# A decode attention block with a gated MLP: TensorE's program made shorter, the first key transpose of unit 1 moved ahead of unit 0's softmax, and the gate moved on VectorE

## The chip, the cores and the metric

One core of one Trainium2 chip runs the kernel. The metric is the device time of one execution in microseconds (us). The kernel before has a median of 111.82 us over 14 runs (111.16 to 113.61).

## The reference

```
x = A_x                                   # [2, 1, 448], bfloat16
xn = layernorm(x)
q = xn @ wq                               # 16 heads of 256
k, v = the last 2048 positions of k_cache, v_cache   # 8 kv heads, each serves 2 q heads
o = softmax(q k^T / 16) v
s = o @ wo                                # [2, 1, 448]
g = silu(relu(xn @ w1) @ w2)              # 448 -> 1792 -> 448
out = x + s * g
```

Two tokens are computed (batch 2), so each weight and each cached key or value is used once or twice: 44 MB are read and hardly any arithmetic is done with them.

## The kernel before

**Units.** The attention is cut into four units, u = 0 to 3: unit u is batch u // 2 and the four kv heads of half u % 2. A unit has 4 MiB of keys and 4 MiB of values. Partition 32h + r holds head h and, for r, 64 neighbouring positions of 256 numbers each (`kv_src`, line 274).

**A unit's work.** VectorE (DVE) transposes the keys in four blocks, `do_T` (376), 32 x 32 at a time, into `kt`. TensorE multiplies each block with the query `qz` in `do_S` (383), eight matmuls in four column tiles, into the bank `sbk`. `softmax` (400) takes the maximum on DVE, the exponential on ScalarE (ACT, 407), a second DVE transpose (409), 16 matmuls that spread the result (413) and a product with a mask (417), which leaves the weights in `pt`; the sum for the denominator is a matmul with `gsum` (420). `do_PV` (426) is 32 matmuls of `pt` with the values. `attend_scale` (443) divides by the sum into `o_sb`; `attend_turn` (448) and `attend_spread` (461) are five small matmuls and two DVE steps that lay the result out in `at_z`, as the stationary operand for wo. `turn_q` (393) writes the next unit's query.

**Loop on TensorE.** `turn(u)` (528) is written four times for the other engines, but TensorE's instructions are put in a loop of four turns by `_Prog.run` (46), with parts in branches (`turn`, `spread`, `pv`, `ffn`), each emitted once. Within the loop a wait is a token: the giver adds to a semaphore and TensorE takes away (102). Turn u does the transposes and scores of unit u, then PV of unit u - 1, then softmax u. PV of unit 3 and the end stand after the loop. A block `pe_visit` (153) is jumped to first and jumps back. All DVE instructions are a single list in the order in which they are written.

**Queries and MLP.** `do_q` (469) needs all of wq and the normalised x (`xr`, 366). `do_H` (483) has x as the stationary operand and w1 as the moving one, in turn 1; its result is clipped, transposed and copied on DVE (491 to 495) and is the stationary operand of `do_F` (509), 14 matmuls on w2 in four column tiles. Their four partial sums are folded at the end (582), and the gate (583, 605 to 608) is computed in a layout of 8 rows by 112 columns.

**The wo product.** `do_wo` (587): nine of the 32 row blocks run as four column tiles into `obk`, are copied (603) and folded into `hbk`; the other 23 add four matmuls of 112 columns each (596). The last two DVE steps (611, 613) make `out_sb`, and ACT's queue writes it.

**Loads.** All large loads are issued by the SP queue, in this order, each behind its wait: wq's first part, K0, wq's rest, K1, V0, w1, w2; K2 (after the scores of unit 0, since K0 and K2 share a buffer); V1 (after PV of unit 0) and K3 (scores of unit 1); V2 (PV of unit 1) and V3 in two parts into the buffer that wq had; then wo in seven parts of 9, 7, 5, 4, 3, 2 and 2 row blocks, after the scores of unit 2, into K0's and K2's buffer.

Of the kernel before, what the change touches and what calls it, by code (L numbers as in the profile page):

```python
# [14 lines left out]
class _Op:  # L15
    __slots__ = ("eng", "fn", "deps", "dma", "needed", "value", "sem", "turn", "group", "token", "gives")

    def __init__(self, eng, fn, deps, dma):
        self.eng, self.fn, self.deps, self.dma = eng, fn, deps, dma
        self.needed, self.value, self.sem = dma, 0, None  # L20
        self.turn, self.group, self.token, self.gives = None, None, None, False


class _Prog:
# [4 lines left out]
    def __init__(self, nc, es):  # L29
        self.nc, self.es = nc, es  # L30
        self.lists = {PE: [], DVE: [], ACTE: [], SP: [], POOL: []}
        self.turn, self.group, self.runs = None, None, {}

    def op(self, eng, fn, deps=(), token=None):
        o = _Op(eng, fn, [d for d in deps if d is not None], False)
        if eng == PE:
            o.turn, o.group, o.token = self.turn, self.group, token
        self.lists[eng].append(o)
        return o
# [6 lines left out]
    def run(self, turns):  # L46
# [6 lines left out]
        taken = {DVE: [], SP: []}  # L53
        for o in pe:
            if o.token is not None:
                assert not o.token.gives
                o.token.gives = True
                taken[o.token.eng].append(o.token)
        for e in taken:
            assert taken[e] == [o for o in self.lists[e] if o.gives]  # L60
# [16 lines left out]
        for e, ops in self.lists.items():  # L77
            sem, count = self.es.enter_context(nc.semaphore(f"s_{e}")), 0
            for o in ops:
                if o.gives:  # L80
                    assert o.dma or not o.needed
                    o.sem = give[e]
# [3 lines left out]
                elif o.needed:  # L86
                    count += 1
                    o.sem, o.value = sem, count
# [22 lines left out]
        for eng, name in ((nc.vector, "dve"), (nc.tensor, "pe")):  # L111
            again[name] = eng.alloc_register(f"{name}_again")
            nc.br("dve_all" if name == "dve" else "pe_visit", engines=[eng.engine])
# [15 lines left out]
        body = [o for o in loop if o.turn == turns - 1]  # L129
        body += [o for o in loop if o.group == "ffn"]  # L130
        with nc.body("pe_all", parent=main, valid_engines=[t.engine]):
            top = nc.cur_bb
# [3 lines left out]
            with t.Fori(0, turns) as i:  # L136
                k = 0
                while k < len(body):
                    g = body[k].group
                    end = next((m for m in range(k, len(body)) if body[m].group != g), len(body))  # L140
                    part, runs = body[k:end], self.runs[g]
                    k = end
                    if runs == list(range(turns)):
                        emit(t, part, seen)
                    elif len(runs) == 1:
                        with t.If(i == runs[0]):
                            emit(t, part, seen)
                    else:
                        assert runs == list(range(runs[0], turns))
                        with t.If(i > runs[0] - 1):  # L150
                            emit(t, part, seen)
            nc.br("pe_past", engines=[t.engine])
            nc.switch_bb("pe_visit", parent=main)
            t.nop()
            nc.br("pe_all", engines=[t.engine])
            nc.switch_bb("pe_past", parent=top)
# [5 lines left out]
def bass_recurrent_scan__sliding_block_cached__dense_activation_relu__decode_kernel(  # L162
# [21 lines left out]
    NU = 4  # L184
# [9 lines left out]
    FIRST = 2  # L194
    NCOL = D // 4
    NROW = 4 * B
    GAP = NROW + 3
    es = contextlib.ExitStack()
    with es:
# [31 lines left out]
        q_n = named("q_n", [128, 512], BF)  # L231
        qz = named("qz", [128, 4 * 64], BF)
        h_n = named("h_n", [128, FC // 4], BF)
        h_t = named("h_t", [128, FC // 4], BF)
        h_z = named("h_z", [128, 14 * GAP], BF)
        x_c = named("x_c", [NROW, NCOL], BF)
        ea = named("ea", [NROW, NCOL], F32)
        g_sb = named("g_sb", [NROW, NCOL], F32)
        tmp = named("tmp", [NROW, NCOL], F32)
# [8 lines left out]
        q_t = named("q_t", [128, 512], F32)  # L248
        ssum = named("ssum", [128, 1], F32)
# [15 lines left out]
        obk_last = psum("obk_last", [128, 512], F32)  # L265
# [13 lines left out]
        d_xc = pr.dma(ACTE, x_c[:, :], A_x[:, 0, :].rearrange("b (i n) -> (b i) n", i=4))  # L279

# [13 lines left out]
        def load_v(u, cuts=(0, NT)):  # L294
            deps = [None if u == 0 else st["q_mm"] if u == NU - 1 else st["PV", u - 1]]
            d_v[u] = []
            for lo, hi in zip(cuts, cuts[1:]):
                d_v[u].append((hi, pr.dma(SP, vbuf[u // (NU - 1)][:, lo * DH:hi * DH],
                                          kv_src(u, A_v_cache)[:, :, lo * DH:hi * DH], deps)))

        d_wq = [pr.dma(SP, wq_sb[:, 0:FIRST * HC], wq_src[:, 0:FIRST * HC])]
        load_k(0)
        d_wq.append(pr.dma(SP, wq_sb[:, FIRST * HC:SLOTS * HC], wq_src[:, FIRST * HC:SLOTS * HC]))
        load_k(1)
        load_v(0)
        st["w1"] = pr.dma(SP, w1_sb[:, 0:W2_AT], w1_src)
        st["w2"] = pr.dma(SP, w2_sb[:, W2_AT:W2_AT + 14 * D].rearrange("p (hf f) -> p hf f", hf=2), w2_src)
# [5 lines left out]
        p_z = [pr.op(POOL, lambda e, t=t: e.memset(t[:, :], 0.0)) for t in (qrep, spread, sel, h_z, at_z)][-1]  # L313

        a_z = [pr.op(ACTE, lambda e, t=t: e.memzero(t[:, :])) for t in (obk, sbk, hbk, fbk, obk_last)][-1]
# [7 lines left out]
        pr.op(ACTE, lambda e: e.activation(tmp[0:B, 0:1], st2[0:B, 0:1], ACT.Exp), [a_sd])  # L323
        for e2 in range(2):
# [39 lines left out]
        for s in range(SLOTS):  # L364
            m_xr = pr.op(PE, mm(mbk_ap(2 * s, 2), xg[0:B, 128 * s + 128:128 * s + 256], ident[0:B, 0:B], s == 0),
                         [v_xn, p_id])
# [56 lines left out]
        def out_bank(u):  # L423
            return obk if u < NU - 1 else obk_last

        def do_PV(u, gs=range(4)):
            bank, src = out_bank(u), vbuf[u // (NU - 1)]
            for g in gs:
                deps, token = [], None
                if u == NU - 1:  # L430
                    deps = [next(d for hi, d in d_v[u] if hi >= 16 * g + 16), st["pt", u]]
                elif g == 0:
                    token = d_v[u][0][1]
                for a in range(2):
                    for i in range(4):
                        t = 16 * g + 4 * i + 2 * a
                        o = pr.op(PE, mm(bank[32 * i:32 * i + 16, :],
                                         pt[:, 8 * t:8 * t + 16], src[:, t * DH:(t + 2) * DH],
                                         g == 0 and a == 0, g == 3 and a == 1, tile_position=(0, 32 * i)), deps, token=token)
                        deps, token = [], None  # L440
            st["PV", u] = o

        def attend_scale(u):
            st["osb", u] = pr.op(DVE, lambda e: e.tensor_scalar(  # L444
                out=o_sb[:, :], in0=view(out_bank(u), 0, [[1, 512]]), scalar1=rs[:, u:u + 1], scalar2=None, op0=ALU.mult),
                [st["PV", u], st["rs", u], st.get(("oT", u - 1))])

        def attend_turn(u):
            deps = [st["osb", u]] if u > 1 else []
            for dhi in range(2):  # L450
                for tp in range(2):
                    o = pr.op(PE, mm(mbk_ap(136 + 8 * dhi, 8), o_sb[:, 256 * tp + 128 * dhi:256 * tp + 128 * dhi + 128],
                                     fold[:, 8 * tp:8 * tp + 8], tp == 0, tp == 1), deps)
                    deps = []
# [6 lines left out]
        def attend_spread(u):  # L461
# [3 lines left out]
                                      [at] if u > 1 else [], token=None if u > 1 else at)  # L465
# [3 lines left out]
        def do_q():  # L469
            deps = d_wq + [v_xr, a_z]  # L470
# [6 lines left out]
            st["q_mm"] = o  # L477
# [5 lines left out]
        def do_H():  # L483
            deps = [st["w1"]]
            for s in range(SLOTS):
                for i in range(4):
                    lo = s * FC + i * (FC // 4)
                    o = pr.op(PE, mm(hbk[32 * i:32 * i + 4, 0:FC // 4], xr[:, 4 * s:4 * s + 4], w1_sb[:, lo:lo + FC // 4],
                                     s == 0, s == SLOTS - 1, tile_position=(0, 32 * i)), deps)
                    deps = []  # L490
            v = pr.op(DVE, lambda e: e.tensor_scalar(
                out=h_n[:, :], in0=hbk[:, 0:FC // 4], scalar1=0.0, scalar2=None, op0=ALU.max), [o])
            v = pr.op(DVE, lambda e: e.transpose(h_t[:, :], view(h_n, 0, [[1, 7], [7, 32]])), [v])
            st["h"] = pr.op(DVE, lambda e: e.tensor_copy(
                view(h_z, 3, [[GAP, 7], [7 * GAP, 2], [4, 2]]), view(h_t, 0, [[32, 7], [2, 2], [1, 2]])), [v, p_z])
# [13 lines left out]
        def do_F():  # L509
            deps = [st["w2"], st["h"]]  # L510
            for f in range(14):
                st["F"] = tiled(fbk, h_z, f, w2_sb, W2_AT + f * D, 4, 10, deps)
                deps = []

        def idle_work(n, deps=()):
            for _ in range(n):
                pr.op(PE, mm(wbk[:, :], ident[:, :], q_n[:, :], True, True), deps)
                deps = ()

        def idle_loop(n, m):  # L520
            def fn(e):
                with e.Fori(0, n):
                    for _ in range(m):
                        o = mm(wbk[:, :], ident[:, :], q_n[:, :], True, True)(e)
                return o
            pr.op(PE, fn)

        def turn(u):
            pr.turn, pr.group = u, "all"
            for blk in range(NBLK):  # L530
                if u:
                    do_T(u, blk)
                if u > 1 and blk in (1, 2):
                    pr.group = "turn" if blk == 1 else "spread"
                    (attend_turn if blk == 1 else attend_spread)(u - 2)
                    pr.group = "all"
# [109 lines left out]
```

## Time and profile before

| | |
|---|---|
| median of 14 runs | 111.82 us |
| the profiled execution | 111.83 us, its span 110.4 us |
| DMA | 44.11 MB, 94.8% of the 16 engines' span, 400 GB/s over it |
| VectorE busy | 63.0 us (57%), 96 instructions |
| TensorE busy | 59.8 us (54%), 552 matmuls |
| ScalarE, GpSimd busy | 10.2 us, 3.1 us |
| TensorE clock granted, mean | 0.86 of full speed |
| a key transpose, 128x2048 | 2.28 us, 16 of them |

The span is the stretch that the profile covers; the rest of an execution's time lies around it. A row of the profile names an instruction's line, engine and tiles, how often it ran, and how long its engine had been idle before it and for what. A line that a helper shares, such as 361 for every matmul, is told apart by its tiles. The chain of waits is followed back from the last instruction: at each step to what released it.

### The profile page before, as it was taken

To read this page: it belongs to the slowest core of one execution; us is meant where nothing else is said; L and a number is where in the kernel's file an instruction comes from. 1 tells how busy PE (TensorE), PEld (TensorE's weight loads), DVE (VectorE), ACT (ScalarE), POOL (GpSimd) and SP (SyncE) were. 2 spreads that over 40 slices of the span, in tenths; PEclk is the share of its full clock that TensorE was granted. 3 is DMA by queue.
4 is the path that set the end of the run, shared out by engine and by line. 5 is a ranking of instruction groups with operands and counts; after the bars stand their busy time and mean duration, and the time that the engine had idled before them with its cause. 6 is when DMAs were issued, how large, how long until landed. Compare 5 with 4: busy or idle time off the path is not lost. (4 is left out here: it accounts for less than half of the span.)

```text
span 110.4 us, 1362 instructions
## 1 busy us (share of the span) xinstructions
PE 59.8 (54%) x552; PEld 19.6 (18%) x558; DVE 63.0 (57%) x96; ACT 10.2 (9%) x19; POOL 3.1 (3%) x11
## 2 busy tenths in 40 slices
PE   0001000075799032999553597992049785888993
PEld 0000000020110030002241010131001022534792
DVE  2049109997200569992586999256399925714601
ACT  4990000000000200000200000020000002000000
POOL 7400000000000000000000000000000000000000
PEclk9999999999769955559998559678558999999999
DMA  3999989998999899998999999899899999899940
GB/s 72 485 389 463 475 358 453 484 428 380 439 487 404 380 397 409 407 520 380 487 451 392 392 523 416 380 428 487 309 439 392 442 428 428 377 423 414 399 178 1
DMA packets 3045, 44.13 MB, mean 400 GB/s; under 512 B 354, under 2 KB 612, under 8 KB 1508
## 3 DMA queue, kind: packets, MB, share of 16 engines
q1 hardware_dynamic: 3008, 44.11, 94.8%
q8 instruction: 1, 0.02, 0.1%
q10 hardware_dynamic: 36, 0.01, 0.0%
HBM read 44.11 MB, written 0.00 MB: 400 GB/s over the span
## 5 line engine op out<-in xcount | busy, mean ns | idle before, releaser
L379 DVE STREAM_TRANSPOSE kt<-kbuf 128x2048 f32<-128x2048 f32 x16 | 35.9, 2286 | 8.6 <-DMA kbuf<-in_A_k_cache_dram 8.6
L361 PE MATMUL sbk<-kt,qz 128*8 128x512 bf16 x128 | 31.1, 1072 | 14.8 <-PEq L102 14.7
L401 DVE TENSOR_REDUCE rm<-sbk 128x1 f32<-128x512 f32 x4 | 2.8, 692 | 14.3 <-PE sbk L361 14.3
L361 PE MATMUL obk<-vbuf,xr 128*4 128x512 bf16 x28 | 3.0, 598 | 14.0 <-DMA vbuf<-in_A_wq_dram 14.0
L407 ACT ACTIVATE et<-sbk,bias 128x512 bf16<-128x512 f32 x4 | 2.7, 687 | 81.2 <-DVE bias L405 81.2
L361 PEld LDWEIGHTS sbk<-kt,qz 128*8 128x8 bf16 x128 | 2.4, 87 | 29.6 <-issue 29.5
L361 PE MATMUL obk<-vbuf,pt 128*16 128x512 bf16 x96 | 6.9, 437 | 0.0
L361 PE MATMUL pbk<-et,spread 128*128 128x32 bf16 x64 | 2.6, 193 | 6.1 <-PEq L102 6.1
L361 PE MATMUL mbk<-ident,xg 2*128 2x2 bf16 x7 | 0.3, 163 | 8.5 <-DVE xg L325 8.5
L361 PE MATMUL hbk<-kbuf,at_z 128*8 128x112 bf16 x92 | 4.8, 213 | 0.0
L409 DVE STREAM_TRANSPOSE et<-et 128x512 bf16<-128x512 bf16 x4 | 2.8, 712 | 3.4 <-ACT et L407 3.4
L417 DVE TENSOR_TENSOR pt<-pbk,hmask 128x512 bf16<-128x512 f32 x4 | 2.8, 692 | 3.3 <-PE pbk L361 3.3
L361 PEld LDWEIGHTS hbk<-kbuf,at_z 128*8 128x8 bf16 x92 | 4.6, 87 | 0.1
L361 PE MATMUL wbk<-q_n,ident 128*128 128x512 bf16 x9 | 3.3, 381 | 2.0 <-DVE qz L396 1.4
L361 PEld LDWEIGHTS obk<-vbuf,pt 128*16 128x16 bf16 x96 | 2.7, 104 | 7.7 <-issue 6.3
L361 PEld LDWEIGHTS pbk<-et,spread 128*128 128x128 bf16 x64 | 2.2, 102 | 9.3 <-issue 9.3
L361 PEld LDWEIGHTS obk<-vbuf,xr 128*4 128x4 bf16 x28 | 0.8, 114 | 15.5 <-issue 15.5
L611 DVE TENSOR_TENSOR tmp<-hbk,g_sb 8x112 f32<-8x112 f32 x1 | 0.3, 262 | 4.4 <-PE hbk L361 4.4
L456 DVE TENSOR_TENSOR at_exp<-mbk,qmask 128x128 bf16<-128x128 f32 x4 | 1.2, 292 | 2.5 <-PE mbk L361 2.5
L361 PE MATMUL obk_last<-vbuf,pt 128*16 128x512 bf16 x32 | 2.3, 380 | 0.3 <-DMA vbuf<-in_A_v_cache_dram 0.3
L322 DVE RECIPROCAL rstd<-sd 2x1 f32<-2x1 f32 x1 | 0.2, 151 | 4.0 <-ACT sd L321 4.0
L444 DVE TENSOR_SCALAR o_sb<-obk,rs 128x512 bf16<-128x512 f32 x3 | 2.2, 731 | 0.0
(80 smaller groups left out, 44.7 us busy)
## 6 DMA issues: line engine op xcount, KB each, us to landing
kbuf<-in_A_k_cache_dram SPq DMA_DIRECT2D x4, 4096.0 KB, 24.1
vbuf<-in_A_v_cache_dram SPq DMA_DIRECT2D x3, 4096.0 KB, 15.6
wf<-in_B_w_dram SPq DMA_DIRECT2D x2, 1568.0 KB, 43.0
vbuf<-in_A_v_cache_dram SPq DMA_DIRECT2D x1, 3072.0 KB, 21.9
vbuf<-in_A_wq_dram SPq DMA_DIRECT2D x1, 2560.0 KB, 20.9
vbuf<-in_A_wq_dram SPq DMA_DIRECT2D x1, 1024.0 KB, 6.2
vbuf<-in_A_v_cache_dram SPq DMA_DIRECT2D x1, 1024.0 KB, 23.7
kbuf<-in_A_wo_dram SPq DMA_DIRECT2D x1, 1008.0 KB, 25.5
```

The source lines that it names most:

```text
L322: v_rs = pr.op(DVE, lambda e: e.reciprocal(rstd[0:B, :], sd[0:B, 1:2]), [a_sd])
L361: return lambda e: e.matmul(out_ap, lhsT=lhsT, rhs=rhs, start=start, stop=stop, skip_group_check=True, **kw)
L379: st["kt", u, blk] = pr.op(DVE, lambda e: e.transpose(view(dst, 0, [[1, 32 * NT]]), view(src, 32 * blk, [[DH // 2, NT], [1, 32]])), [d_k[u ...
L401: v = pr.op(DVE, lambda e: e.tensor_reduce(out=rm[:, :], in_=sbk[:, :], axis=AX.X, op=ALU.max), [st["S", u, NBLK - 1]])
L407: a = st["exp", u] = pr.op(ACTE, lambda e: e.activation(e_sb, sbk[:, :], ACT.Exp, bias=bias[:, 0:1], accum_out=ssum[:, 0:1]), [v, st.get(( ...
L409: token = pr.op(DVE, lambda e: e.transpose(e_t, e_sb), [a, st.get(("Pt", u - 1))])
L417: st["pt", u] = pr.op(DVE, lambda e: e.tensor_tensor(out=view(pt, 0, [[8, NT], [2, 4], [1, 2]]), in0=view(pbk, 0, [[2, NT], [0, 4], [1, 2] ...
L444: st["osb", u] = pr.op(DVE, lambda e: e.tensor_scalar(out=o_sb[:, :], in0=view(out_bank(u), 0, [[1, 512]]), scalar1=rs[:, u:u + 1], scalar ...
L456: st["at", u] = pr.op(DVE, lambda e: e.tensor_tensor(out=view(at_exp, 0, [[16, 8], [8, 2], [1, 8]]), in0=view(mbk, 136, [[1, 8], [8, 2], [ ...
L611: v_t = pr.op(DVE, lambda e: e.tensor_tensor(out=tmp[:, :], in0=hbk[0:NROW, 0:NCOL], in1=g_sb[:, :], op=ALU.mult), [m_o, v_g])
```

## The change

- **Program of TensorE.** The block that was visited first is gone. The loop runs six turns instead of four, with its parts in the order `turn`, `ffn`, `s`, `pv`, `softmax`, each in a branch: PV of unit 3 and the last two attend steps are turns 4 and 5 of the loop. The matmuls for `xr` and H become loops over the seven slots with computed addresses. More waits of TensorE become tokens.
- **First transpose of unit 1.** In turn 0 `do_T(1, 0)` is issued after the scores of unit 0 and ahead of softmax 0; turn 1 transposes blocks 1 to 3 only. `attend_turn` and `attend_spread` of unit u - 2 now stand ahead of turn u's transposes and scores instead of between them.
- **MLP.** H has w1 as the stationary operand (128 columns, seven elements apart) and runs right after q; one DVE step clips its result into `h_z` behind the second transpose of unit 0. F is 14 matmuls of 448 columns in one tile and moves to turn 4. The gate works on 2 rows by 448 columns, and on DVE it stands behind the copy of wo's first sums and ahead of `o_sb` of unit 3.
- **wo.** The first nine blocks and their fold are in turn 4 (`early_wo`), in a bank of their own. The others are two matmuls of 224 columns in two column tiles. Output and x are two rows at partition 0 and two at 32, and the output is written by two DMAs, from ACT and SP.
- **Loads.** wq in one piece, w1, K0, K1, V0, K2, V1, K3, V2, w2, wo's first part, V3 (in the buffer of the other V, after PV of unit 2), wo's other parts. V0 to V2 get a second, 64-byte load for the second token.
- **Fillers.** Two matmuls on a spare bank ahead of each softmax's matmuls and two behind them; a filler loop of two rounds ahead of PV 3 (five before).

```
-        d_wq = [pr.dma(SP, wq_sb[:, 0:FIRST * HC], wq_src[:, 0:FIRST * HC])]
+        d_wq = pr.dma(SP, wq_sb[:, 0:SLOTS * HC], wq_src)
+        st["w1"] = pr.dma(SP, w1_sb[:, 0:W2_AT], w1_src)
         load_k(0)
-        d_wq.append(pr.dma(SP, wq_sb[:, FIRST * HC:SLOTS * HC], wq_src[:, FIRST * HC:SLOTS * HC]))
         load_k(1)
         load_v(0)
...
         def do_H():
+            def body(e, s):
+                for j in range(7):
+                    o = mm(view(hbk, 64 + 4 * j, [[1, 4]]), view(w1_sb, FC * s + j, [[7, 128]]), view(xr, 4 * s, [[1, 4]]), False)(e)
+                return o
+            return looped(SLOTS, body, [st["w1"]])
...
         def do_F():
             deps = [st["w2"], st["h"]]
             for f in range(14):
-                st["F"] = tiled(fbk, h_z, f, w2_sb, W2_AT + f * D, 4, 10, deps)
+                st["F"] = pr.op(PE, mm(view(fbk, 0, [[1, D]], n=B), view(h_z, f * GAP + 3, [[4, 2]]),
+                                       w2_sb[:, W2_AT + f * D:W2_AT + f * D + D], f == 0, f == 13), deps)
+            st["a_e"] = pr.op(ACTE, lambda e: e.activation(ea[0:B, :], g_ap, ACT.Exp, scale=-1.0), [st["F"]])
+        def gate():
+            v_d = pr.op(DVE, lambda e: e.tensor_scalar(
+                out=ea[0:B, :], in0=ea[0:B, :], scalar1=1.0, scalar2=None, op0=ALU.add), [st["a_e"]])
+            v_rc = pr.op(DVE, lambda e: e.reciprocal(tmp[0:B, :], ea[0:B, :]), [v_d])
+            for t in range(2):
+                st["g"] = pr.op(DVE, lambda e, t=t: e.tensor_tensor(
+                    out=g_sb[32 * t:32 * t + B, :], in0=fbk[0:B, NCOL * t:NCOL * t + NCOL], in1=tmp[0:B, NCOL * t:NCOL * t + NCOL],
+                    op=ALU.mult), [v_rc, p_z])
...
         def turn(u):
+            pr.turn = u
+            if u > 1:
+                pr.group = "turn"
+                attend_turn(u - 2)
+                attend_spread(u - 2)
+            if u > NU:
+                pr.turn, pr.group = None, None
+                return
+            if u == NU:
+                pr.group = "ffn"
+                do_F()
+                early_wo()
+                gate()
+                idle_loop(FILL, 2)
+            if u < NU:
+                pr.group = "s"
+                for blk in range(NBLK):
+                    if u > 1 or u == 1 and blk:
+                        do_T(u, blk)
+                    do_S(u, blk)
+                if u == 0:
+                    do_T(1, 0)
             if u:
                 pr.group = "pv"
                 do_PV(u - 1)
+            if u < NU:
+                pr.group = "softmax"
+                between(2)
+                softmax(u)
+                between(2)
+            pr.turn, pr.group = None, None
             if u:
                 attend_scale(u - 1)
             if u < NU - 1:
                 turn_q(u + 1)
...
         load_v(2)
-        load_v(3, (0, 48, 64))
+        load_w2()
+        turn(3)
         d_wo, j0 = {}, 0
         for n in WO_PARTS:
             v, j = divmod(j0, NWO)
             d_wo[j0] = pr.dma(SP, wo_sb[:, j0 * D:(j0 + n) * D], wo_src[v, :, j * D:(j + n) * D], [st["S", 2, NBLK - 1]])
+            if j0 == 0:
+                load_v(3)
             j0 += n
+        turn(NU)
+        turn(NU + 1)
+        j0 = TILED
+        for n in WO_PARTS[1:]:
+            deps = [d_wo[j0], st["at_z", 3]]
+            for j in range(j0, j0 + n):
+                for t in range(2):
+                    m_o = pr.op(PE, mm(view(hbk, 0, [[1, NCOL]], n=B, p0=32 * t), view(at_z, j * GAP + 3, [[4, 2]]),
+                                       wo_sb[:, j * D + NCOL * t:j * D + NCOL * t + NCOL], False, tile_position=(0, 32 * t)), deps)
+                    deps = []
+            j0 += n
```

## The prediction

> **What bounds the kernel now.** I read the chain of waits first, then the DMA queues, then busy time by stage over the last microseconds, then the landing records.
>
> ```profile
> 75.91 25.55 DMA kbuf<-in_A_wo_dram
> 101.45 0.04 issue
> 101.50 0.73 PE obk L361 x9
> 102.23 0.16 issue
> 102.39 0.59 PE wbk L361 x2
> 102.98 5.54 PE hbk L361 x100
> ```
>
> The end hangs on a transfer: the first part of wo lands at 101.45, and from there TensorE runs to 108.5. Before that one wait of 25.55 us covers a queue, not an engine.
>
> ```profile
> q1 hardware_dynamic: 3008, 44.11, 94.8%
> q8 instruction: 1, 0.02, 0.1%
> HBM read 44.11 MB, written 0.00 MB: 400 GB/s over the span
> ```
>
> The packets fill 94.8% of the 16 engines' span; in the view by slices every one from the second to the 38th of 40 is at 0.8 or above. So the kernel is bound by moving 44.11 MB; the landing records give 9.73 us for each 4.19 MB of K or V (w2 at 49.82, K2 at 59.54, V1 at 69.27), 431 GB/s, with no hole that compute caused.
>
> ```profile
> 104.00:105.00 1.00, 1.00 (x25) 1.00 (x22) 0.17 (x1) 0.00 (x0) 0.00 (x0) 1.00 1.02 395
> 105.00:106.00 1.00, 1.00 (x25) 1.00 (x22) 0.00 (x0) 0.00 (x0) 0.00 (x0) 1.00 0.83 309
> 106.00:107.00 1.00, 1.00 (x24) 1.00 (x22) 0.00 (x0) 0.00 (x0) 0.00 (x0) 1.00 0.28 102
> 107.00:108.00 1.00, 1.00 (x23) 0.89 (x19) 0.00 (x0) 0.00 (x0) 0.00 (x0) 1.00 0.05 18
> ```
>
> (stage: length, busy us of PE, PEld, DVE, ACT, POOL, granted clock, DMA share, GB/s.) From 105 the DMA share falls to 0.83, 0.28, 0.05: a few engines finish late. The landing records say which. Each transfer counts as landed when all 16 engines have reported, and one engine trails from the start: the first wq part landed at 5.79 on the second slowest and 6.94 on the slowest, K1 at 31.32 and 32.50, the last wo part at 107.91 on the slowest. In the packet records one engine takes a 16,384-byte instruction packet at 2.59 for 0.92 us, and one engine's first data packet begins at 3.49, when the others begin at 1.74 to 2.33. I take these to be the same engine: **an instruction fetch costs one engine, and so every landing, 1.17 us.**
>
> **What the skill says.** "Runtime: NRT & Kernel Launch", Instruction fetch mechanics: instructions come in blocks of 16 KiB, 256 instructions, over a DMA queue of the sequencer's own; a taken branch out of the resident blocks forces a fetch. The trace agrees with one packet of that size. "DMA: Bandwidth & Descriptors", on the increment by 16: a transfer runs on up to 16 engines that finish independently, and only the full count means landed; the 1.17 us shows it. "TensorE: Matmul & The Clock Gate", Part 1: an idle window of some 3.4 us halves the clock. Agrees: 32 PV matmuls took 1.92 us and, at 71 us, 2.89. "TensorEngine Tiling (Array Packing)", Key Properties: column tiles work in parallel. Agrees: 1.92/32 is 60 ns for 512 columns.
>
> **The change, part by part.** Times are in the changed kernel unless "now" is said.
>
> *The fetch.* I count TensorE's program now: 331 matmuls of two instructions and some 50 others, about 710, three blocks. After: xr 1, q 28 and 1, H 7, turn 5, F 14, early wo 9, fold 4, filler 6, S 32, PV 32, softmax 18, tail 46: 203, or 406 instructions, and 60 to 100 waits, branches and address steps: 466 to 506, below 512, two blocks. Now the visit to a late block at 1.2 us meets no delay, so two blocks are resident and the fetch is for the third. Without it the slowest engine is the second slowest: landings 1.17 us earlier. Bounds: 0 (the fetch stays, or the end of the program still needs a block) and 1.17; I take 1.17.
>
> *Order of loads.* The bytes are the same. wq and w1 come ahead of K0, w2 (1.6 MB, 3.8 us) moves behind V2, and wo's first part ahead of V3. With the fetch gone: K1 at 31.32 + 3.77 (w1) = 35.1; K0 at 25.4; w1 15.6; wq 11.9. V0, K2, V1, K3, V2 follow each 9.73 later, if they are issued in time. The three tiny added loads are 4 bytes on each engine: below 0.1 us.
>
> *Unit 0 and 1.* T(0,*) from 25.4: 8.89 (four transposes now) + 0.2 for the relu = 34.5; the last S 2.12 later, 36.6 (now 49.79 to 51.91). The moved transpose waits for K1 at 35.1 and ends at 37.4: softmax(0) is held 0.8 us, but 2.28 us leave the chain behind it. Softmax to the second qz takes 4.80 (now 36.11 to 40.91): 42.2. Three transposes 6.7: 48.9. Last S: 51.0. PV and V1's issue 1.75 (now 51.94 to 53.69), first packet 1.0 later (now 0.74 to 1.74): **53.8, and the queue is empty at 35.1 + 19.46 = 54.6.** No hole, 0.8 us spare. Now w1 and w2 stood ahead of K2, so moving w2 away spends 3.8 us of cover.
>
> *Units 2 and 3.* Softmax to o_sb 5.13 (now 51.97 to 57.10), qz 0.5, then turn and spread, which now hide between transposes, stand alone for some 0.9; H and F's DVE steps (0.38 + 0.53 + 0.21 us) are gone. T(2) 57.7 to 66.6, last S 68.7; V2 issued by 71.6, needed at 74.0. T(3) 75.4 to 84.3, last S 86.4, PV2, V3 issued at 88.2 warm or 89.3 cold, first packet 89.2 to 90.3. Now V3 has a buffer of its own and waits only for q; after, it waits for PV2, and wo's six other parts stand behind that wait on SP, where they would land later than V3 anyhow. Its queue is empty at 35.1 + 48.65 + 3.8 + 2.5 = 90.0. **Hole 0 to 0.3 us; I take 0.2.** Loop branches may add 0.1 to 0.3 each unit: up to 1 us more.
>
> *H.* 7 x 7 loads of 128 columns with a step of 7. Each at least 0.10 us (the 128x128 loads of spread, 102 ns), 5 us; at most 4 times that, as S's strided reads stand to PV's (246 to 60 ns), 20 us. It starts at 15.9; S may start as late as 30.0 (37.4 less four S in a row, 7.37 now) before the moved transpose no longer hides it: 14 us, 0.29 us each. I take 0.15 each, hidden.
>
> *Gate and F.* Softmax(3) to at_z(2): 86.4 + 5.13 + 1.3 = 92.8. F is 14 x 0.187 us one after the other (448 columns at the warm 0.42 ns that 213 ns for 512 give): 2.6 plus 0.2, 95.4; early wo 0.75, the copy 0.62: 96.7. Then on DVE, behind the wait for ACT's exponential (96.1, so no wait): add 0.55, reciprocal (0.84 now for 112, 0.15 for one, so 6.2 ns each) 2.95 for 448, two products 0.38 each (0.26 for 112, 0.69 for 512): **the gate ends at 101.0.** Behind it in DVE's queue stands o_sb(3). V3's rest lands at 106.75 - 6.45 = 100.3 (wo's other parts took 101.46 to 107.91), PV ends at 100.95: they meet, and nothing is lost.
>
> *End.* o_sb(3) to at_z(3) 1.94 now: 103.0. 46 matmuls on two column tiles, 224/2.4/2 = 47 ns each, 2.3 us: 105.4, so they wait for the last part. Now 100 matmuls took 5.54 from 102.98. Bounds for the 46: 47 ns each and, without overlap, 93: 4.3 us, 107.3. Last landing: 107.91 - 1.17 + 0.2 = 106.95. Four matmuls and their drain 0.37: 107.3. Two DVE steps of 224 at 0.38 with gaps: 108.15 (now 0.26 each, +0.24). Issue and write 1.30 as now, 0.05 for the second queue: 109.5, and 0.2 because several times meet here: **span 109.7.** The profiled run has 111.83 around 110.4, 1.43 outside, and stands at the median of 111.82: 111.1, 0.6% faster.
>
> *Fillers, masks.* Fillers run while TensorE waits; cold, two cost 0.85 us ahead of softmax(2)'s sums: 0 to 0.5. The sixth clear on ACT moves xr by 0.5 us to about 11.2, ahead of wq.
>
> **Rivals.** *The fetch stays or moves to the loop (0.22):* 1.17 us back, 112.2; for it, that blocks also hold code around the program. *The gate holds o_sb(3), slower (0.20):* if F runs at half clock it takes 5.2 us and the gate ends at 103.6; o_sb(3) to at_z(3) 105.6, 46 matmuls 2.3 (4.6 cold): 107.9 to 110.2 instead of 106.95. It decides once the gate ends later than about 102.6. Middle: 112.6. For it: the clock was 0.5 in 76 to 84; against: 1.0 from 84 on, with the same S and PV ahead. *V3 or S late, slower (0.15):* branches and fillers of 0.3 per step, or H above 0.29 us a load, open a hole of 2 us: 113.1. *A smoother end (0.06):* now 76 to 80 moved 344 GB/s, some 0.7 us lost; without that, 110.3. My forecast: 0.37.
>
> **How the numbers follow.** A measurement tells 0.5%, 0.56 us. Forecast and smoother end give faster 0.40, the first rival mostly the same, the others slower. Their bounds, 110.3 and 113.1, are the range; the forecast's own is 110.5 to 111.6, and signs are mixed.
>
> **What would show it.** No 16,384-byte packet and 16 landings within 0.6 us (step one); V1 and V3 first packets within 1 us of the queue's end; o_sb(3) started by the PV matmuls, not by DVE's own queue; the last matmuls waiting for wo. A DMA share below 0.9 between 53 and 56 or 89 and 92, or DVE busy with the reciprocal past 102, would make it wrong.

## The result and the profile after

The changed kernel takes 114.03 us in the median of 10 runs (113.06 to 115.75); the kernel before took 112.18 in the same comparison (47 runs). The ratio is 1.020, with a 95% interval of 1.016 to 1.023: **2.0% slower**, where 0.6% faster had been forecast. Ratios, here and below, leave out executions more than 1.5% above the fastest of the same kernel, so this one is not the quotient of the two medians. The profiled execution took 114.62 us around a span of 111.9; in the other runs 1.4 to 1.6 us lie outside the span.

The chain of waits ends as it did before, on a transfer (start, us, what; the last lines):

```profile
94.10 15.19 DMA kbuf<-in_A_wo_dram
109.29 0.04 issue
109.33 0.38 PE hbk L360 x4
109.71 0.02 issue
109.73 0.40 DVE tmp L629
```

But now it is the last part of wo that TensorE waits for, with four matmuls behind it instead of 100. That was forecast, with 106.95 for the landing; it came at 109.29. These 2.3 us hold all by which the profiled span misses its forecast (111.9 for 109.7). The page's queues tell the same:

```profile
span 111.9 us, 1427 instructions
q1 hardware_dynamic: 2964, 44.11, 93.8%
q8 instruction: 1, 0.02, 0.1%
HBM read 44.11 MB, written 0.00 MB: 394 GB/s over the span
```

The bytes are the same and the rate is lower, 394 for 400 GB/s. And one instruction packet is still there, though TensorE's program of 456 instructions fits two blocks. (A second one comes behind the span, at 113.43, in this execution, which has 2.7 us outside.) By stage (length, busy us of PE, PEld, DVE, ACT, POOL, granted clock, DMA share, GB/s), first of the kernel before:

```profile
53.00:56.00 3.00, 1.64 (x42) 1.11 (x38) 1.29 (x4) 0.78 (x2) 0.00 (x0) 1.00 0.88 382
89.00:92.00 3.00, 3.00 (x40) 0.84 (x32) 1.23 (x4) 0.00 (x0) 0.00 (x0) 1.00 1.01 434
```

and of the kernel after:

```profile
53.00:56.00 3.00, 1.57 (x21) 0.84 (x20) 1.94 (x4) 0.20 (x2) 0.00 (x0) 1.00 0.70 208
89.00:92.00 3.00, 2.03 (x33) 1.03 (x26) 1.28 (x4) 0.78 (x2) 0.00 (x0) 1.00 0.81 314
...
107.00:108.00 1.00, 1.00 (x22) 0.71 (x18) 0.00 (x0) 0.00 (x0) 0.00 (x0) 1.00 0.99 358
108.00:109.00 1.00, 0.73 (x12) 0.27 (x10) 0.00 (x0) 0.00 (x0) 0.00 (x0) 1.00 0.14 48
```

These are the two places that the prediction named as its own test, a share below 0.9 between 53 and 56 or 89 and 92. Both falls are there. The line of 0.9 was a loose one, since the kernel before has 0.88 at 53 to 56; but 0.70 with 208 GB/s is far below that. Each fall belongs to the issue of a V transfer (start, us, engine; SPq is the queue of SyncE):

```profile
52.77 0.54 SPq L45 DMA_DIRECT2D vbuf<-in_A_v_cache_dram  x1
53.35 0.59 SPq L45 DMA_DIRECT2D nil<-in_A_x_dram  x1
53.98 0.53 SPq L45 DMA_DIRECT2D kbuf<-in_A_k_cache_dram  x1
...
89.61 1.20 SPq L45 DMA_DIRECT2D vbuf<-in_A_v_cache_dram  x2
```

V1 is issued at 52.77, as forecast (52.8). In the packet records 15 of the 16 engines run out of K2 at 53.3 to 54.2. On 14 of them V1's first packet begins at 54.09 to 54.48 and takes 1.7 to 2.2 us instead of the 1.22 that a 32 KB packet takes in a running stream. So such an engine idles up to 1.2 us, then loses 0.5 to 1.0 on its first packet.

One engine trails: after an instruction packet at 38.98 (1.06 us) one engine's V0 lands 0.94 behind all others. (Records don't name the engine; which belong together is read from their times.) This slowest engine sets every landing that TensorE waits for. It was busy with K2 until 55.11, and still its V1 landed 11.53 after its K2 (55.54 to 67.07), where an uninterrupted V takes 9.73. It restarted too: its first packet of V1 begins at about 56.25, 1.1 us after its last of K2, and takes 1.99.

At 90 to 92 V3 meets most of the engines empty again, but not the slowest one: that has wo's first part until 92.6 and goes on without a break. The large part of V3 takes it 7.41 us, and 7.31 uninterrupted.

"DMA: Bandwidth & Descriptors", Latency and other measured facts, gives 0.6 us to the first byte for this kind of issue and up to 2 us for an access to HBM under high load. Here the first packet came 0.78 us after the end of the issue (53.31 to 54.09), 1.33 after its beginning, so the measured lead is the longer one. The slow first packets are within the second number, but no run here shows their cause.

**Theory A:** both V transfers are issued into a queue that has just run dry, because unit u's V waits for PV of unit u - 1; each restart costs over 1 us. **Theory B:** such falls are absorbed, and something else sets the end: TensorE at half clock, the gate on DVE, or the program's fetch.

### The profile page after: what moved, and what is told of

The parts are those of the page before. It is cut to its first block, busy times and chain, and to the rows that moved or that the text cites. A ratio compares the mean times of both kernels' runs of the same rounds, so it can differ in the third digit from the quotient of the medians.

```text
span 111.9 us, 1427 instructions
## 1 busy us (share of the span) xinstructions
PE 68.4 (61%) x520; PEld 22.5 (20%) x526; DVE 64.7 (58%) x94; ACT 10.9 (10%) x20; POOL 3.5 (3%) x13
## 5 line engine op out<-in xcount | busy, mean ns | idle before, releaser
L360 PE MATMUL mbk<-ident,xg 2*128 2x2 bf16 x7 | 1.2, 178 | 11.8 <-DVE par L329 9.0
L360 PE MATMUL hbk<-xr,wf 128*128 x49 | 6.8, 208 | 2.5 <-issue 2.5
L360 PE MATMUL obk<-vbuf,pt 128*16 128x512 bf16 x128 | 7.9, 381 | 0.0
L360 PEld LDWEIGHTS hbk<-xr,wf 128*128 x49 | 6.2, 131 | 3.3 <-issue 3.0
L360 PE MATMUL wbk<-spread,ident 128*128 128x512 bf16 x14 | 5.1, 411 | 0.8 <-issue 0.8
L360 PEld LDWEIGHTS obk<-vbuf,pt 128*16 128x16 bf16 x128 | 3.5, 93 | 7.9 <-issue 5.6
L360 PE MATMUL fbk<-wf,h_z 128*2 128x448 bf16 x14 | 4.4, 495 | 0.2 <-issue 0.2
L360 PE MATMUL mbk<-fold,o_sb 128*128 128x8 bf16 x16 | 1.0, 166 | 4.3 <-PEq L105 4.3
L360 PE MATMUL hbk<-kbuf,at_z 128*2 128x224 bf16 x46 | 2.9, 258 | 1.0 <-DVE at_z L464 0.5
L516 DVE RECIPROCAL tmp<-q_t 2x448 f32<-2x448 f32 x1 | 2.9, 2941 | 0.0
```

The source lines that it names most:

```text
L360: return lambda e: e.matmul(out_ap, lhsT=lhsT, rhs=rhs, start=start, stop=stop, skip_group_check=True, **kw)
L516: v_rc = pr.op(DVE, lambda e: e.reciprocal(tmp[0:B, :], ea[0:B, :]), [v_d])
```

## The experiments

Ratios are to the kernel before, run on the same chip. "Landing" is that of wo's last part on its slowest engine: 107.91 before, 109.29 after. Most ratios below rest on few runs and their intervals overlap, and a landing is that of one execution.

### One part undone or shifted at a time

**wo's first part with 16 blocks.** It adds 1.9 us of transfer ahead of V3, and so cover for the second restart.

```
-    WO_PARTS = [9, 7, 5, 4, 3, 2, 2]
-    TILED = 9
+    WO_PARTS = [16, 5, 4, 3, 2, 2]
+    TILED = 16
```

> Theory of the empty queue: the changed kernel loses some 1.3 us at V1 and again at V3, because each is issued when the DMA queue has just run dry. Here 16 of wo's row blocks (1.8 MB) instead of 9 stand ahead of V3, 1.9 us more cover: the fall in DMA throughput at 90 to 92 goes, the one at 53 to 56 stays, the last landing comes 1.2 us earlier (near 108.1 instead of 109.3), the time is near 112.8, 0.6% above before. Rival, the gate: the end hangs on DVE, where the gate ahead of o_sb of unit 3 ends at 104; V3 lands no earlier or later here, so 114.0 or more.

Ratio 1.038 (1.031 to 1.046), 116.42 us, yet a span of only 111.4: 4.9 us lie outside it. The fall at 89 to 92 is gone (440 GB/s) and the landing is 107.67. But this isn't the cover alone: the program has 442 instructions of TensorE instead of 456, and its one instruction packet lies behind the end, at 114.1, so that no engine trails from V0 on. So I made it 456 again, with seven more filler matmuls in the program ahead of PV 3 (nine in one round, for two in each of two rounds):

```
-                idle_loop(FILL, 2)
+                idle_loop(1, 9)
```

> As the run with 16 row blocks ahead of V3, with nine fillers in place of four ahead of PV of unit 3, so that TensorE's program is as long as in the changed kernel (456 instructions instead of 442). Theory: the 442-instruction program paid some 3.4 us outside its span (4.9 instead of 1.5) for a block of instructions that is fetched only when the program ends; here it is fetched in the loop again, at 39, and the time is the span + 1.5: 112.6 to 112.9. The empty queue: no fall at 90 to 92, last landing near 108. Rival, the 3.4 us belong to the load of 1.8 MB in one piece: 116.4 again.

Ratio 1.013 (1.007 to 1.018), span 112.2, 1.7 us outside: the shorter program had cost the other 3.2 us. The second fall is gone:

```profile
89.00:92.00 3.00, 1.61 (x22) 0.84 (x20) 1.89 (x4) 0.24 (x2) 0.00 (x0) 1.00 1.02 436
```

The landing is 108.53, 0.76 earlier than in the kernel after. But all of this is there at V1 already (66.30 for 67.07); from V1's landing to the last one both take 42.2 us. So the second fall had cost the slowest engine next to nothing. And the last matmuls end at 110.04, behind the landing:

```profile
107.05 2.98 PE L360 MATMUL hbk<-kbuf,at_z 128*2 128x224 bf16 x32 [0.49 <-DVE at_z L464]
```

32 matmuls in 2.98 us are 93 ns each; at full clock, further down, they take 53. With the stream earlier a second limit shows, so part of theory B holds as well.

**V in halves,** the first half issued behind half of PV:

```
-            lo = 48 if u == NU - 1 else NT
+            lo = NT // 2
+            first = [st["PVh", u - 1] if u else None]
```

> V loads in two halves, the first issued after half of the PV matmuls, about 0.95 us sooner (and without the tiny extra loads). Theory of the empty queue: the fall at 53 to 56 goes or shrinks to a third, K3 lands 1.0 to 1.3 us sooner, V3 is issued 2 us sooner and its fall goes as well: 112.0, level with before. The gate: no change, 114.0, or 0.4 more since 16 matmuls instead of 8 are behind V3's last landing.

Ratio 1.012 (1.002 to 1.021). V1 is issued at 52.04, 0.73 earlier, and the rate at 53 to 56 is 273 instead of 208. It didn't help the trailing engine: its V1 lands at 67.80 (after: 67.07), and the fall at 89 to 92 stays (274 GB/s). The 112.0 that theory A gave is missed, at 113.67. **V in pieces of 16, 32 and 16 of the 64 positions,** with wo's 16 blocks and 456 as well:

> In addition V loads in three pieces (16, 32 and 16 rows of a partition's 64), the first issued after a quarter of the PV matmuls, 1.4 us sooner. Theory of the empty queue: V1's first packets at 52.6 to 53.0, ahead of the typical engine's end at 53.5, so neither fall remains; last landing 107.1, the end 2.4 later, 111.1 in all, 0.9% faster than before. If only the fetch or the gate mattered: 112.8 as the run without the pieces.

Ratio 1.018 (1.012 to 1.024): V1's first piece is issued at 52.58, the landing is 108.93, and 32 matmuls at half clock (3.17 us) end at 110.70. The fall at 53 to 56 is still there (210 GB/s), against the expectation: the issue came 0.2 us earlier than in the kernel after, not 1.4. Issuing 0.2 to 0.7 earlier isn't enough.

**The first transpose of unit 1 back in turn 1:**

```
-                    if u > 1 or u == 1 and blk:
+                    if u:
...
-                if u == 0:
-                    do_T(1, 0)
```

> The first transpose of unit 1 goes back behind softmax 0. Theory of the empty queue: the chain from K1 to V1's issue is 1.5 us longer (2.28 less the 0.8 that the transpose held softmax 0), V1's hole grows by 1.5 us: 115.5, 3% above before. Rival, the moved transpose does harm by holding softmax 0: 113.2.

Ratio 1.012 (1.004 to 1.020), 113.22 us: no slower than the kernel after, where theory A gave 115.5. The rival's 113.2 is met, but not its reason, since V1 is issued 1.44 later than in the kernel after, not earlier. The fall is deep:

```profile
53.00:56.00 3.00, 2.18 (x42) 0.94 (x35) 1.43 (x5) 0.78 (x2) 0.00 (x0) 1.00 0.38 98
89.00:92.00 3.00, 2.08 (x30) 0.95 (x22) 1.42 (x4) 0.71 (x2) 0.00 (x0) 1.00 1.20 507
```

But V1 lands at 66.76 on its slowest engine, no later than 67.07: the 15 others merely lost their lead. For the same reason the second fall is gone: V3 is issued at 89.28, when these others still have wo's first part (its median landing is 92.2, for 90.9 in the kernel after). So a hole counts only as far as it reaches the slowest engine, and a fall in the mean rate overstates it.

**w2 back ahead of K2,** 3.8 us of cover for V1:

```
+        load_w2()
...
         load_v(2)
-        load_w2()
```

> w2 (1.6 MB) goes back ahead of K2, the rest as changed. Theory of the empty queue: V1 has 3.8 us more cover and its fall goes, but K3 lands 2.5 us later, V3 is issued as much later, and its queue runs dry at the same byte: the fall at 90 to 92 is 3 us long instead of 1: 114.5. If V1's hole alone counted: 112.7. The gate: 114.0.

Ratio 1.031 (1.022 to 1.040). The fall is moved, not removed:

```profile
53.00:56.00 3.00, 1.57 (x22) 0.84 (x20) 1.94 (x4) 0.20 (x2) 0.00 (x0) 1.00 0.94 404
89.00:92.00 3.00, 3.00 (x42) 0.95 (x34) 1.23 (x4) 0.50 (x1) 0.00 (x0) 1.00 0.07 30
```

V1 now lands 9.74 behind K2, but K3 comes later, V3 is issued at 91.85 into a queue that is empty on all engines, its large part takes the slowest one 10.73 us instead of 7.31, and the landing is 110.90. That is theory A's effect, larger than expected (115.8 us for 114.5).

**The visited block put back** (`pe_visit`, 459 instructions):

> The block that is jumped to first is put back into the changed kernel. Theory: the 16,384-byte packet moves from 39 back to 2.6, one engine trails by 1.2 us from the start, every landing that is waited for is 1.2 us later, V1 and V3 are issued 1.2 us later, and their falls are that much longer on the other 15 engines: 114.7 to 115.2. Rival, where the fetch lies is all the same: 114.0.

Ratio 1.012 (1.006 to 1.018). The instruction packet moves to 2.00, one engine trails from the start as it did before the change, and no fall is left at 89 to 92 (471 GB/s). Longer falls and 114.7 to 115.2 us had been expected, but V1's restart cost the slowest engine only 0.9 us here (10.61 from K2 to V1), and why is open. The landing is 108.14, but o_sb(3) waits 0.7 us for the gate, whose F had run at half clock, and then

```profile
105.75 4.45 PE L366 MATMUL hbk<-kbuf,at_z 128*2 128x224 bf16 x46 [0.77 <-DVE at_z L470]
```

sets the end at 110.2, two microseconds behind the landing.

**The kernel before with V3 in the other V's buffer,** behind PV of unit 2 and wo's first part:

```
-            deps = [None if u == 0 else st["q_mm"] if u == NU - 1 else st["PV", u - 1]]
+            deps = [st["PV", u - 1] if u else None]
...
-            bank, src = out_bank(u), vbuf[u // (NU - 1)]
+            bank, src = out_bank(u), vbuf[0]
...
```

> The kernel before with one part of the change alone: V3 goes into the buffer of the other V and waits for PV of unit 2, behind wo's first part. Theory of the empty queue: PV of unit 2 ends at 92.3, V3's first packets come at 93.7, the queue is empty from 90.4: a fall of 3.3 us, and 0.8 more for the slow first packets: 115.5 to 116.2. Rival, a V in its own buffer is worth nothing since the DMA engines catch up later: 112.1.

Ratio 1.056 (1.049 to 1.062), 118.90 us: V3 issued at 93.04, 105 GB/s at 89 to 92, landing 111.92. The one wait costs the old kernel more than the whole change cost, and more than expected (116.2 at most), partly because its end behind the landing is longer here: 5.2 us, for 2.5.

### The wait taken away: a second V buffer

The buffer that held wq is free after q. V1 and V3 go there; V1 then waits for q, V2 and V3 for the PV two units back. TensorE's PV is emitted twice, once for each buffer (525 instructions).

```
-            deps = [st["PV", u - 1] if u else None]
-            d_v[u] = [pr.dma(SP, vbuf[0][:, 0:lo * DH], kv_src(u, A_v_cache)[:, :, 0:lo * DH], deps)]
+            deps = [st["PV", u - 2] if u > 1 else st["q_mm"] if u else None]
+            d_v[u] = [pr.dma(SP, vbuf[u % 2][:, 0:lo * DH], kv_src(u, A_v_cache)[:, :, 0:lo * DH], deps)]
...
-                pr.group = "pv"
+                pr.group = f"pv{u % 2}"
```

> The kernel after with V1 and V3 in the buffer that held wq, as a second V buffer: V1 then waits for q alone and V3 for the PV of unit 1, so that neither is issued into an empty queue. TensorE's PV is emitted twice for it, once for each buffer (525 instructions instead of 456). Theory A (the two restarts of an empty queue, 1.3 us each on a typical engine and 1.8 in all on the trailing one, are what moved the last landing): no fall of the rate at 53 to 56 nor at 90 to 92; V1 lands 9.73 after K2 on the slowest engine, wo's last part at 107.3 to 107.7 instead of 109.3, span 110.0 to 110.8, 111.8 to 112.4 us. Theory B (the restarts are absorbed, and the loop's slower turn or TensorE's half clock sets the end): the falls go, but the end of TensorE stays at 109.5 or later: 113.5 to 114.5. A third block of program in the loop can be fetched again in each turn: each fetch costs one engine 0.95 more; if that happens on one engine, the landings move by as much.

Ratio 0.996 (0.991 to 1.001), **111.69 us**, a span of 110.1 and a landing of 107.33. Both falls are gone:

```profile
53.00:56.00 3.00, 1.67 (x22) 0.84 (x20) 1.85 (x4) 0.28 (x2) 0.00 (x0) 1.00 0.92 393
89.00:92.00 3.00, 1.54 (x24) 1.02 (x24) 1.74 (x5) 0.00 (x0) 0.00 (x0) 1.00 1.08 464
```

V1 lands 9.72 behind K2 (55.62 to 65.34) on the same trailing engine, with the same instruction packet (39.04). The landing is the one that theory A gave (107.3 to 107.7). With wo's 16 blocks on top (511 instructions):

> The same, and wo's first part with 16 blocks instead of 9, so that 32 matmuls are left for the end instead of 46 (511 instructions). Theory A: landings as in the run with two V buffers, 107.3 to 107.7, and V3 lands near 102.0, later by 7 blocks of wo; at_z of unit 3 near 105, 32 matmuls 1.5 us warm (106.5) or 3.1 at half clock (108.1): 111.8 to 112.6. Theory B: 113.5 to 114.5, with TensorE at half clock at the end. If the program of 525 is fetched in the loop and this one of 511 is not, the two differ by about 1 us.

111.70 us, ratio 0.999 (0.996 to 1.003): the same.

**The waits put back by themselves,** with the code of the two buffers: V1 behind PV of unit 0, V3 behind PV of unit 2, both.

```
-            deps = [st["PV", u - 2] if u > 1 else st["q_mm"] if u else None]
+            deps = [st["PV", u - 2] if u > 1 else st["PV", 0] if u else None]
...
+            deps = [st["PV", u - 1] if u > 2 else st["PV", u - 2] if u > 1 else st["q_mm"] if u else None]
...
+            deps = [st["PV", u - 1] if u else None]
```

V1's wait:

> The version with two V buffers at 111.69 us, with one added wait: V1 is issued behind the PV of unit 0, as in the kernel after, though its buffer is free. Theory (each restart of an empty queue costs by itself): V1 issued at 52.8, the fall at 53 to 56 is back, the trailing engine's V1 lands at 66.9 instead of 65.3, all later landings 1.6 later, no fall at 90: last landing 108.9, span 111.5 to 111.8, 113.1 to 113.5 us. Rival (the first fall is absorbed behind the trailing engine, only the second costs): V1 at 65.3 to 65.8, 111.7 to 112.2.

V3's wait:

> The version with two V buffers, with one added wait: V3 is issued behind the PV of unit 2. Nothing is lost at 53 here, so K3 lands at 75.1 on the slowest engine instead of 76.8, and V3 is issued near 87.9; the queue ends at 88.5 to 89.3 on typical engines and 91.0 on the trailing one, first packets at 89.2. Theory: a fall of 0 to 0.7 us on typical engines, nothing on the trailing one; last landing 107.3 to 108.0: 111.7 to 112.4 us. Rival (the restart costs 1.3 us also on an engine that is still busy): last landing 108.6, 113.0.

Both:

> The version with two V buffers (525 instructions, PV emitted twice), with both waits put back: the same data flow as the kernel after, with the code of the two buffers. Theory: as after, falls at 53 to 56 and 90 to 92, last landing 109.0 to 109.4, 113.6 to 114.3 us. Rival (the gain came from the other code or the longer program): 111.7 to 112.5.

V1's wait: 113.24 us in the profiled execution; the four runs lie between 111.97, as fast as without the wait, and 114.9, too wide for a ratio. V1 at 66.61 (+1.27), K3 at 76.32 (+1.26), landing 109.17. (0.6 of that is lost at w2, 82 to 88, without a hole.) V3's wait: 112.40, ratio 1.011 (1.002 to 1.019), landing 108.40. Both: 113.38, ratio **1.020 (1.012 to 1.028)**, the 1.020 of the kernel after, with a landing of 108.62. So neither the other code nor 525 instructions instead of 456 had a part in the gain. The windows of the three, in this order:

```profile
53.00:56.00 3.00, 1.84 (x23) 0.88 (x22) 1.67 (x4) 0.47 (x2) 0.00 (x0) 1.00 0.65 251
89.00:92.00 3.00, 1.92 (x26) 0.95 (x22) 1.58 (x4) 0.55 (x2) 0.00 (x0) 1.00 1.09 462
```

```profile
53.00:56.00 3.00, 1.60 (x22) 0.84 (x20) 1.92 (x4) 0.22 (x2) 0.00 (x0) 1.00 0.97 415
89.00:92.00 3.00, 1.53 (x24) 1.03 (x24) 1.79 (x4) 0.00 (x0) 0.00 (x0) 0.92 0.85 295
```

```profile
53.00:56.00 3.00, 1.63 (x22) 0.84 (x20) 1.88 (x4) 0.26 (x2) 0.00 (x0) 1.00 0.62 197
89.00:92.00 3.00, 1.87 (x26) 0.91 (x22) 1.64 (x4) 0.49 (x2) 0.00 (x0) 1.00 0.99 324
```

Each wait makes its own fall and leaves the other place whole. V3's wait moved the landing by 1.1 us where 0 to 0.7 was expected: the trailing engine lost 0.7 on it though it was busy until 91.4, and the other 0.3 was there at V0, where its instruction packet had cost more.

What each restart took from the slowest engine (us; from one landing to the next; uninterrupted 9.73 and 7.31):

| | K2 to V1 | wo's first part to V3's large part | last landing |
|---|---|---|---|
| kernel after | 11.53 | 7.41 | 109.29 |
| wo with 16 blocks, 456 instructions | 10.62 | 7.31 | 108.53 |
| two buffers | 9.72 | 7.33 | 107.33 |
| two buffers, V1's wait | 10.87 | 7.31 | 109.17 |
| two buffers, V3's wait | 9.71 | 8.03 | 108.40 |
| two buffers, both waits | 10.84 | 7.41 | 108.62 |

So the two costs don't add, and theory A's "over 1 us" for each holds for V1's restart only. Behind V1's restart the slowest engine is so late that V3 is issued in time for it, and V3's costs 0.1; by itself it costs 0.7. Of the 1.96 us between the landing of the kernel after and that with two buffers, 1.73 are there at V1 (67.07 and 65.34). This is so in the profiled executions: others of these kernels have spans that are over a microsecond longer, and their landings aren't recorded.

### The half clock at the end

Seven fillers in the end chain: three ahead of the wait for o_sb (in every turn from the second), one between turn and spread, three ahead of the wait for at_z(3).

```
+                between(3)
                 attend_turn(u - 2)
+                between(1)
                 attend_spread(u - 2)
...
+        between(3)
         j0 = TILED
```

With wo's 16 blocks, instead of the seven fillers ahead of PV 3:

> wo's first part with 16 blocks (as in the run at 113.65), and seven filler matmuls in the end chain instead of the seven more ahead of PV 3: three ahead of the wait for o_sb, one between turn and spread, three ahead of the wait for at_z (456 instructions as after). In the run at 113.65 the 32 last matmuls took 2.99 us at a granted clock of 0.5 and ended at 110.04, 1.5 after wo's last landing at 108.53. If the half clock set that end: the matmuls take 1.5 to 1.6 us, end at the last landing plus 0.2, 108.7: span 110.9, 112.3 to 112.7 us. If the clock isn't what sets it (the fillers only delay the chain): no gain, 113.5 to 114.

Ratio 1.010 (1.006 to 1.013). The 32 matmuls take 1.70 us instead of 2.98, but V3 landed at 103.86 and PV 3 itself ran at half clock (3.51 us), so the matmuls began 0.9 later and the end moved by 0.4 only. With the visited block, and the gate behind at_z(3) on DVE:

> The kernel after with the visited block back (as in the run at 113.87, where the program's fetch lies at 2.0 us), the gate moved on DVE behind at_z of unit 3, and the seven fillers in the end chain. There o_sb of unit 3 waited 0.7 us for the gate, and 46 matmuls took 4.5 us at half clock and ended at 110.2, 2.1 after the last landing at 108.1. If gate and clock set that end: o_sb at 102.5, at_z at 104.6, 46 matmuls 2.2 us, the last ones after the landing at 108.1; the gate ends at 108.7; span 110.5 to 110.9, 112.0 to 112.4. If the landing at 108.1 was early by chance (the fall at 90 back): 113 to 114.

Ratio **1.007 (1.003 to 1.010)** instead of 1.012 (the intervals overlap), 112.63 us where at most 112.4 was expected, span 111.1:

```profile
105.85 2.34 PE L366 MATMUL hbk<-kbuf,at_z 128*2 128x224 bf16 x42
108.38 0.36 PE L366 MATMUL hbk<-kbuf,at_z 128*2 128x224 bf16 x4 [0.20 <-DMA kbuf<-in_A_wo_dram]
```

The end is the landing (108.34) again: clock and gate together had been worth 1.3 us of the span there. And with two V buffers:

> The version with two V buffers, with seven filler matmuls in the end chain. There 46 matmuls took 3.97 us at a granted clock of 0.5 to 0.6 and ended at 107.9, with wo's last landing at 107.33. Warm: 2.3 us, the last four after the landing at 107.7: span 109.8 instead of 110.1, 111.3 to 111.5 us. If the clock doesn't matter any more: 111.6 to 111.8. If the longer program is fetched again in the loop: 112 to 112.5.

111.81 us, ratio 1.003 (1.001 to 1.005). The 46 matmuls, 3.97 us at half clock without fillers, now wait for the landing, but in that run it came at 107.86; from landing to the end of the span went 2.64 us instead of 2.77. The clock is worth 0.1 there, and the expected 111.3 to 111.5 is missed.

## Why the prediction was wrong, step by step

- **The fetch** (1.17 us earlier, bounds 0 and 1.17): failed. The packet at 2.59 went away, and all landings up to K1 came as forecast (35.17 for 35.1). But a packet came at 38.98, inside the loop, and from V0 on one engine trailed 0.95. The first rival, the fetch in the loop, named this; its 112.2 us misses the rest. With fewer instructions (442) it moved behind the end and cost more. The step from this to the end was weak, too: in the kernel before the slowest engine is 1.1 behind the second up to K3 (78.98 and 77.87), but from V2 on by 0.06 (89.17 and 89.11; at the end 107.91 and 107.85), since another engine had fallen as far back. So 1.17 came off the last landing only if that loss didn't come again.
- **The order of loads:** right, to 0.1 us up to K1; from V0 on the slowest engine is 1.0 late by the fetch, until the first restart.
- **"First packet 53.8, and the queue is empty at 54.6. No hole, 0.8 us spare": this step failed.** The issue was right to 0.03 us. Three terms were not. The queue's end was taken from a landing on the slowest engine, and 15 of the engines run dry at 53.3 to 54.2. From issue to first packet it was 1.33 instead of 1.0, which had been read at the start of the kernel. And the restart's slow packets, up to 1.0 us, weren't in the sum at all, nor that the engine with work left would restart as well. It lost 1.8 us, and the run with V1's wait alone puts the step at 1.3 us at K3.
- **"Hole 0 to 0.3 us; I take 0.2":** the hole was larger on most engines, for the same reasons and since K3 came 1.4 later than forecast (T(3) at 76.80 for 75.4) and V3 was issued at 89.61. On the slowest engine it cost 0.1 in the kernel after, so the 0.2 is near by luck: the first restart had made room for it. By itself it costs 0.7. The two waits together are 2.0% against 0.4% *faster* without them.
- **H hidden:** right: 17.8 to 27.1, 131 ns a load (taken: 150). 0.46 us for each turn of its loop was not counted, and nothing waited for it.
- **The gate** (rival at 0.20): F did run at half clock, 4.4 us, and the gate ended at 104.04, past the 102.6 from which it was to decide. It held o_sb(3) by 0.5 us, but the landing was later still, so it decided nothing in the kernel after; in the run with the visited block it was 0.7 of the path.
- **The end:** right in kind. Four matmuls and their drain 0.38 (0.37 forecast), DVE 0.40 and 0.38 (0.38 each). From landing to the end of the span 2.6 us (2.75 forecast).
- **The third rival,** V3 or S late by a hole of 2 us, 113.1 at 0.15, was nearest in mechanism. But the hole that counted was V1's, which it doesn't name, and it came neither from branches nor from H: V1's issue was on time and H hidden. 114.03 is beyond it.

With both waits gone the kernel takes 111.69, 0.6 above the forecast of 111.1, with a landing of 107.33 for 106.95. That is nearer than the sum deserves, by luck: the fetch still costs 0.96, and against it stand the 0.2 for a hole and about 0.45 at V2, which takes 9.75 us there and took 10.19 in the kernel before, whose last landing the sum began from.

**Left open:** why the trailing engine, with work until 55.1 and V1 issued 2.3 us ahead of that, also paused 1.1 us, and why its loss at V1 lies between 0.85 and 2.3 us in the runs with this restart, without following the time of the issue (52.04 to 54.21); and why w2 took 4.17 to 4.45 us instead of 3.83 in three runs without a late issue.

## What to carry to other kernels

A transfer that waits for a buffer should be issued before the first of the engines runs dry, not before the slowest lands. Here it needs 1.3 us of lead, and a late one cost the slowest engine from 0.7 to 3.8 us (V3's wait alone; the kernel before with it), or next to nothing where an earlier hole had already put that engine behind. So count cover for each wait from the packet records of a typical engine, in microseconds, and ask which later wait pays when bytes are moved from one place to another. Two buffers that alternate took the question away here. A gain in the stream shows only down to the next limit, so look at what the compute chain behind the last input would do at half clock.

## What the runs showed of the hardware

- A restarted queue: 1.33 us from the beginning of the issue to the first packet, and 1.7 to 2.2 us for a first 32 KB packet that takes 1.22 in the stream (kernel after, V1). An engine that still had 1.8 us of work at the end of that issue paused 1.1 us all the same.
- One 16 KB instruction packet in the loop (1.03 to 1.08 us) makes one of 16 engines 0.8 to 1.4 us late, and with it the landings that follow, until a restart or another loss evens the engines out (0.94 in the kernel after); "Runtime: NRT & Kernel Launch", Instruction fetch mechanics, has the fetch on a DMA queue of its own, and the trace agrees that there is one, but its time is taken from the data.
- TensorE's program with 442 instead of 456 instructions had that packet behind the end and 4.9 instead of 1.7 us outside the span.
- 224-column matmuls on two column tiles: 53 to 59 ns each at full clock (32 in 1.70 us, 42 in 2.34 and 2.47), 93 to 97 at half clock (32 in 2.98, 46 in 4.45).
